# Chunk attention and feed-forward on one core: the first two tiles of attention in quadrant form, with their order written out step by step

## Chip, core and metric

One core of a Trainium2 chip runs the kernel alone. The metric is the device time of one execution in microseconds; the kernel before has a median of 288.91 us over 3 runs (288.83 to 289.1).

## What is computed

q, k and v have 8 batches, 8 heads, 576 rows and a head size of 64, in float32. Each head's rows are cut into 9 chunks of 64 and attention stays within a chunk. The heads are then joined to 4608 tokens of width 512, which go through a feed-forward network of width 2048 with an exact GELU.

```python
    scores = scale * np.matmul(q_c, k_c.transpose(0, 1, 2, 4, 3))
    ...
    attn = np.exp(scores)
    attn = attn / (np.sum(attn, axis=-1, keepdims=True) + 1e-09)
    out = np.matmul(attn, v_c)
    ...
    h = x @ w_in
    ...
    g = 0.5 * h * (1.0 + erf(h * inv_sqrt2))
    return (g @ w_out).astype(np.float32)
```

## The kernel before

**Tiles.** The work is 9 tiles of 512 tokens: tile t below 8 is the first 512 rows of batch t, tile 8 the last chunk of all batches. Heads go in 4 pairs g; the 512 columns of a pair are 8 chunks of 64. A tile has three parts: its attention, which gives x (128 x 4 x 512); mm1 (`mm1_slot`, L402), which makes the 16 slots f of h with 4 matmuls each over the slices ks of x, and the GELU on ScalarE (L405); and mm2 (`mm2_slot`, L418), which sums the 16 slots of h into 4 blocks of output rows. `phase(t)` runs mm1 and mm2 of tile t, and the attention of tile t+1 stands between its mm2 matmuls. For that, `extra2` says which pieces go ahead of which step. The program is a manual schedule: every engine works through its own queue in the order in which the program names its instructions.

**Attention of tiles 2 to 8** is in quadrant form (`quad_S`, `quad_av`): q and k are turned by a DMA transpose, V lies with keys on the partitions, and each matmul uses a 64x64 quarter of TensorE (L228, L280), so that four run at once. The change leaves it as it is.

**Attention of tile 0** comes first of all. SyncE issues the loads of q and k pair by pair (L114), then those of V (`load_v`, L163, eight DMAs into half of the partitions each), then w_in (L509). VectorE casts q to bfloat16 (L170) and GpSimd casts k and V (L170, L174). TensorE turns q and k by 128x128 transposes (L181); VectorE copies q out (L187). k goes into block-diagonal tiles k_bd, two copies of half the partitions on ScalarE (L194), and V into v_bd, so that a matmul over all 128 partitions does both heads of a pair (`att_S` L297, `att_av` L371). The zero blocks are memset by VectorE and GpSimd (L72 to L77). Row sums come from a matmul with ones (L305), a 32x32 transpose, a reciprocal and another transpose on VectorE (L309 to L314) for pairs 0 and 1, and from small matmuls (L349), a reciprocal (L352), float32 matmuls that spread it (L358) and a copy (L362) for pairs 2 and 3. VectorE multiplies A.V by the reciprocals into x (L373). `keep_warm` puts matmuls on zeros between them. Then come the casts of w_in (L512) and w_out (L520), shared by GpSimd and VectorE, and the first two f slots of mm1, slice by slice.

**Attention of tile 1** lies in tile 0's mm2, which there runs by h slot (`mm2_rows`, L472): for every f one matmul for each of the four row blocks, up to f 11, then by row block (L418). It has the same block-diagonal form, with the sums of pairs 1 to 3 in one bank (`att_sums`, L323). ScalarE carries the reciprocals over the partitions in small copies (L334). The last A.V stands between the first matmuls of tile 1's mm1, which does three f slots at once, in this order:

```python
        for ks in range(KS):
            for u in between.get(ks, ()):
                u()
            for a in range(n):
                nc.tensor.matmul(h_ps[a][:], w_in_sb[:, ks, (f + a) * P:(f + a + 1) * P], st["x"][:, ks, :],
                                 start=(ks == 0), stop=(ks == KS - 1))
```

**Buffers.** Every load lands in one of 6 stage tiles and waits for the casts that last read it. SyncE keeps at most eight of its DMAs in flight, since each waits for the eighth before it. TensorE's results use 8 banks, in three pools: `ps_mm` 3, `ps_tp` 2, `ps_at` 3.

## Time and profile before

| | |
|---|---|
| median of 3 runs | 288.91 us |
| profiled execution, own time | 289.0 us |
| its span | 287.2 us |
| TensorE, ScalarE, VectorE, GpSimd busy | 97%, 62%, 40%, 29% of the span |
| mm1 and mm2 matmuls (L402, L418, L472) | 576, 512 and 48, 379 ns each in the rows |
| DMA, read from HBM and written | 36.70 MB, 9.44 MB |

A matmul's row shows issue to end, and the next is issued before that end: in a steady stretch they follow each other every 0.216 us. In rows of a timeline the numbers are start, length, engine, line, operation, tiles and shape; in brackets stands the idle time before it and what ended that. Windows give per engine the busy time and the count of instructions, then the granted clock of TensorE, the mean busy share of the 16 DMA engines, and GB/s.

### The profile page before, as it was taken

What the parts mean: (1) busy time and instruction counts of PE and PEld (TensorE: products, weight loads), DVE (VectorE), ACT (ScalarE), POOL (GpSimd) and SP (SyncE); (2) the same over time, 40 slices, a digit from 0 to 9 for tenths busy, and PEclk for the clock granted to TensorE, in tenths of its full rate; (3) what the DMA queues carried; (4) which work ended last, traced back from release to release, by engine and by line L of the source; (5) the groups of instructions that cost most, each with busy time, mean ns of one, the idle gap of its engine ahead of it and who ended that gap; (6) DMA issues with size and microseconds to landing.
All of it is one profiled execution on the core that took longest, in us unless ns stands there. A gap on an engine that the chain in (4) does not pass through costs nothing.

```text
span 287.2 us, 5795 instructions
## 1 busy us (share of the span) xinstructions
PE 277.8 (97%) x2317; PEld 133.2 (46%) x2317; DVE 114.0 (40%) x209; ACT 176.8 (62%) x359; POOL 82.6 (29%) x134
## 2 busy tenths in 40 slices
PE   6699999999999999999999999999999999999995
PEld 2464455444444444444444444444444444444444
DVE  5855259504910491039202930293019401940011
ACT  3766757967647763677367737863686378646400
POOL 6759677511620620161005200620015020000000
PEclk9999999999999999999999999999999999999999
DMA  7999997999999926991698259924996490030033
GB/s 211 234 337 402 391 368 179 248 282 248 221 284 289 233 83 184 283 211 48 179 284 193 79 160 270 223 81 130 199 157 125 120 264 2 2 146 0 2 73 73
DMA packets 119435, 53.86 MB, mean 188 GB/s; under 512 B 97776, under 2 KB 112368, under 8 KB 119408
## 3 DMA queue, kind: packets, MB, share of 16 engines
q1 hardware_dynamic: 119248, 53.36, 71.0%
q8 instruction: 18, 0.29, 0.4%
q10 hardware_dynamic: 160, 0.13, 0.2%
q14 instruction: 9, 0.07, 0.1%
HBM read 36.70 MB, written 9.44 MB: 161 GB/s over the span
## 4 chain that ended last, share of the span: by engine, by line
PE 82%; DMA 10%; DVE 3%; SPq 1%; ACT 1%; issue 1%; POOL 0%; DVEq 0%
PE h_ps L402 38%; PE y_ps L418 38%; DMA arrival<-in_moe_w_out_dram 8%; DMA arrival<-in_k_dram 2%; PE s_ps L228 2%; PE av_ps L280 2%; PE y_ps L450 1%; SPq L114 1%; DVE x L373 1%; PE rc_ps L358 1%; DVE rc L341 1%; PE y_ps L472 1%; ACT k_bd L194 0%; ACT pT L299 0%; PE av_ps L371 0%
## 5 line engine op out<-in xcount | busy, mean ns | idle before, releaser
L402 PE MATMUL h_ps<-x,w_in_sb 128*128 128x512 bf16 x576 | 126.1, 379 | 0.7 <-POOL w_in_sb L512 0.6
L405 ACT ACTIVATE h<-h_ps 128x512 bf16<-128x512 f32 x144 | 85.5, 597 | 60.8 <-PE h_ps L402 60.7
L418 PE MATMUL y_ps<-w_out_sb,h 128*128 128x512 bf16 x512 | 113.8, 379 | 0.0
L402 PEld LDWEIGHTS <-w_in_sb 128*128 128x128 bf16 x576 | 56.2, 98 | 68.4 <-POOL w_in_sb L512 0.7
L418 PEld LDWEIGHTS <-h 128*128 128x128 bf16 x512 | 48.7, 98 | 57.0 <-issue 0.2
L246 DVE STREAM_TRANSPOSE pt<-pT 128x256 f32<-128x256 f32 x28 | 12.2, 437 | 106.8 <-ACT pT L235 106.8
L170 POOL CAST q_nat<-arrival 128x512 bf16<-128x512 f32 x31 | 18.0, 620 | 95.7 <-DMA arrival<-in_q_dram 71.8
L206 POOL CAST v_nat<-arrival 128x1024 bf16<-128x1024 f32 x14 | 14.5, 1040 | 39.5 <-DMA arrival<-in_v_dram 27.0
L536 ACT ACT_TABLE_LOAD x18 | 23.1, 1283 | 1.0 <-PEq L681 0.7
L433 DVE COPY y_sb<-y_ps 128x512 f32<-128x512 f32 x11 | 7.6, 690 | 36.7 <-PE y_ps L418 33.0
L259 ACT COPY part<-part 32x32 f32<-32x32 f32 x56 | 12.3, 219 | 15.0 <-DVE part L249 14.5
L287 DVE TENSOR_TENSOR x<-av_ps,rc 128x512 bf16<-128x512 f32 x28 | 18.9, 676 | 2.2
L249 DVE TENSOR_REDUCE part<-pt 128x16 f32<-128x512 bf16 x28 | 19.2, 685 | 1.0
L168 POOL CAST k_nat<-arrival 128x512 bf16<-128x512 f32 x28 | 16.2, 612 | 0.9 <-DMA arrival<-in_k_dram 0.8
L433 ACT COPY y_sb<-y_ps 128x512 f32<-128x512 f32 x24 | 13.8, 580 | 0.9
L235 ACT ACTIVATE pT<-s_ps 128x512 bf16<-128x512 f32 x28 | 14.3, 593 | 0.0
L472 PE MATMUL y_ps<-w_out_sb,h 128*128 128x512 bf16 x48 | 11.8, 379 | 0.4 <-POOL w_out_sb L520 0.4
L194 ACT COPY k_bd<-tp 64x512 bf16<-64x512 bf16 x12 | 6.9, 578 | 6.7 <-PE tp L181 6.5
L273 DVE STREAM_TRANSPOSE rc<-rb 128x512 f32<-128x512 f32 x14 | 9.9, 707 | 0.2
L273 DVE STREAM_TRANSPOSE rc<-across 128x512 f32<-128x512 f32 x14 | 9.8, 701 | 0.0
L174 POOL CAST v_bd<-arrival 64x512 bf16<-64x512 f32 x14 | 8.6, 615 | 0.7
L520 POOL CAST w_out_sb<-arrival 128x512 bf16<-128x512 f32 x10 | 6.7, 701 | 4.4 <-DMA arrival<-in_moe_w_out_dram 4.4
(76 smaller groups left out, 151.0 us busy)
## 6 DMA issues: line engine op xcount, KB each, us to landing
out_dram<-y_sb SPq DMA_DIRECT2D x32, 256.0 KB, 2.2
arrival<-in_v_dram SPq DMA_DIRECT2D x58, 128.0 KB, 3.4
arrival<-in_k_dram SPq DMA_DIRECT2D x28, 256.0 KB, 6.3
arrival<-in_q_dram SPq DMA_DIRECT2D x7, 1024.0 KB, 6.5
arrival<-in_moe_w_out_dram SPq DMA_DIRECT2D x4, 1024.0 KB, 12.9
arrival<-in_moe_w_in_dram SPq DMA_DIRECT2D x6, 512.0 KB, 7.1
arrival<-in_v_dram SPq DMA_DIRECT2D x28, 64.0 KB, 2.5
arrival<-in_q_dram SPq DMA_DIRECT2D x4, 256.0 KB, 5.0
```

Of the source, the lines that this page charges most:

```text
L168: copy(st[nm][:, :, g], st[nm + "f"][:, :, g].rearrange("p (q r) d -> p q r d", r=2))
L170: copy(st[nm][:, g].rearrange("p j r d -> p r j d"), st[nm + "f"][:, 2 * g:2 * g + 2])
L206: copy(st["v"][:, r::2], st["vf"][:, r::2])
L249: nc.vector.tensor_reduce(st["part", g2][:, c, :, :, 0], pt[:].rearrange("p n e u -> p n u e"), axis=mybir.AxisListType.X, op=mybir.AluOpT ...
L273: nc.vector.transpose(rc[:], tiles[t]["rb", g2][c].to_broadcast([P, NB, 32]))
L287: nc.vector.tensor_tensor(x.rearrange("p n (e u) -> p n e u", u=2), st["av"][g2][c][:].rearrange("p n (e u) -> p n e u", u=2), st["rc", 2 ...
L402: nc.tensor.matmul(h_ps[a][:], w_in_sb[:, ks, (f + a) * P:(f + a + 1) * P], st["x"][:, ks, :], start=(ks == 0), stop=(ks == KS - 1))
L405: nc.scalar.activation(st["h"][:, f + a, :], h_ps[a][:], Act.Gelu)
L418: nc.tensor.matmul(y_ps[:], st["h"][:, f, ms * P:(ms + 1) * P], w_out_sb[:, f, :], start=(f == 0), stop=(f == FF - 1))
L433: (AC if ms < 3 and t + 1 < NT else DV)(y_sb[:], y_ps[:])
L472: nc.tensor.matmul(tiles[t]["y_ps", ms][:], tiles[t]["h"][:, fi, ms * P:(ms + 1) * P], w_out_sb[:, fi, :], start=(fi == 0), stop=False)
L536: nc.scalar.activation(act_scratch[:], rest[:, 0:1], func)
```

## The change

- **Tiles 0 and 1 in quadrant form.** k stays dense: one copy out of the transposes (`att_T`) instead of two halves, and no k_bd, v_bd or memsets for them. `att_S` and `att_av` use 64x64 quarters. `att_S` takes one pair in tile 0 (16 matmuls, two Exp of 128x256), two in tile 1 (32 matmuls, two Exp of 128x512). V is loaded by head into all partitions (`load_v`) and cast by pair.
- **Reciprocals of two pairs.** `pair_sums` gives the sums of pairs 0 and 1 (tile 1: also 2 and 3) with two matmuls of 32 columns, one transpose and one reciprocal on half the partitions. `pair_over` spreads them with one float32 matmul, 128x32, where ScalarE copied; `pair_rc` makes the factors from that bank. In tile 0 pairs 2 and 3 keep small matmuls (`att_sums`, `att_spread`). The last step, `att_x`, is two instructions of half the width for each pair.
- **mm1 by slice.** `mm1_first` does the first f slots of tile 0 (two) and tile 1 (four, was three) ks by ks, with the last A.V between the slices: one pair in tile 0, two in tile 1.
- **Order.** Tile 0: GpSimd casts all of q and k and sets up four constants behind q 0 (`both` takes eight small copies); each piece is named where it is to run. SyncE issues V of heads 4 to 7 after the first half of w_in's first part; w_in's parts 2 and 3 are one DMA each; w_out's part 1 and tile 1's k come in halves. The stage has 7 tiles. Tile 1's pieces stand at other steps; ScalarE does all four y copies of tile 0; the fourth store of tile 0 follows V of tile 2.

The removed lines can be seen in the functions above; here stand the lines that are added and those kept between them.

```diff
+    both = consts.tile([P, P], f32, name="both")
+    nc.gpsimd.memset(both[:], 0.0)
+    for s in range(G):
+        for a in range(2):
+            at0 = CH * (s % 2) + QD * a
+            nc.gpsimd.tensor_copy(both[QD * s:QD * (s + 1), at0:at0 + QD], ident[QD * s:QD * (s + 1), QD * s:QD * (s + 1)])
...
-    stage = ctx.enter_context(tc.tile_pool(name="stage", bufs=6))
+    stage = ctx.enter_context(tc.tile_pool(name="stage", bufs=7))
...
+    def load_v(t, heads):
+        for h in heads:
+            nc.sync.dma_start(v_arrival(t)[:, h], v[t, h, 0:MT, :].rearrange("(n key) d -> key n d", key=P))
...
+    def att_T(t, nm, g, copy):
+        tp = ps_tp.tile([P, J, P], bf16, tag="tp", name="tp")
         for j in range(J):
+            nc.tensor.transpose(tp[:, j], tiles[t][nm][:, g, j].rearrange("p r d -> p (r d)"), ident[:])
+        to = work.tile([P, CT, CH], bf16, tag=nm + "T", name=nm + "T", bufs=4)
+        copy(to[:].rearrange("p i (c j) -> p i c j", j=J), tp[:].rearrange("p j (i c) -> p i c j", i=CT))
+        tiles[t][nm + "T", g] = to
...
+    def pair_sums(t, g2, pool, tag):
+        hold = slice(CH * g2, CH * (g2 + 1))
+        sum_ps = pool.tile([P, MT], f32, tag=tag, name="sums_ps")
+        for r in range(2):
+            at0 = CH * g2 + QD * r
+            nc.tensor.matmul(sum_ps[at0:at0 + QD], ones_c[:], tiles[t]["pT", 2 * g2 + r][:].rearrange("p u e -> p (u e)"),
+                             start=True, stop=True, tile_position=(0, at0))
+        t1 = work.tile([P, NB, 32], f32, tag="t1", name="t1", bufs=1)
+        nc.vector.transpose(t1[hold], sum_ps[hold].rearrange("p (n e) -> p n e", e=32))
+        r1 = work.tile([P, 2, NB], f32, tag="r1", name="r1", bufs=2)
+        nc.vector.reciprocal(r1[hold], t1[hold].rearrange("p n (c e) -> p c n e", c=2)[:, :, :, 0])
+        tiles[t]["r1", g2] = r1
+    def pair_over(t, g2, pool, tag):
+        hold = slice(CH * g2, CH * (g2 + 1))
+        rb = pool.tile([P, 2, NB], f32, tag=tag, name="rb_ps")
+        nc.tensor.matmul(rb[:], both[hold], tiles[t]["r1", g2][hold], start=True, stop=True, tile_position=(CH * g2, 0))
+        tiles[t]["rb", g2] = rb
+    def pair_rc(t, g2, c):
+        rc = work.tile([P, NB, 32], f32, tag="rc", name="rc", bufs=4)
+        nc.vector.transpose(rc[:], tiles[t]["rb", g2][:, c].to_broadcast([P, NB, 32]))
+        rows = rc[:].rearrange("p n e -> p (n e)").rearrange("p (u e) -> p u e", e=CH)
+        for g in (2 * g2, 2 * g2 + 1):
+            half = CT // 2
+            tiles[t]["rc", g, c] = rows[:, half * (g % 2):half * (g % 2 + 1)]
...
+    def att_S(t, gs, pool, tag):
+        st = tiles[t]
+        g2, half = gs[0] // 2, CT // 2
+        s_ps = [pool.tile([P, CT, CH], f32, tag=tag, name="s_ps") for _ in range(2)]
+        if gs[0] % 2 == 0:
+            for r in range(2):
+                st["pT", 2 * g2 + r] = work.tile([P, CT, CH], bf16, tag="pT", name="pT", bufs=5)
+        for g in gs:
+            for n in range(half):
+                for a in range(2):
+                    for r in range(2):
+                        c = a ^ r
+                        rs, cs = slice(CH * r, CH * (r + 1)), slice(CH * c, CH * (c + 1))
+                        nc.tensor.matmul(s_ps[r][cs, half * (g % 2) + n, :], st["kT", g][rs, 2 * n + c],
+                                         st["qT", g][rs, 2 * n + c], start=True, stop=True,
+                                         tile_position=(CH * r, CH * c))
+        for r in range(2):
+            u = slice(half * (gs[0] % 2), half * (gs[-1] % 2 + 1))
+            nc.scalar.activation(st["pT", 2 * g2 + r][:, u], s_ps[r][:, u], Act.Exp, scale=scale)
...
+    def att_sums(t, g, pool, tag):
+        st = tiles[t]
+        half = CT // 2
+        sT = pool.tile([P, half // 2, 2, 2], f32, tag=tag, name="sT")
+        for a in range(half // 2):
+            for r in range(2):
+                u = half * (g % 2) + 2 * a
+                nc.tensor.matmul(sT[:, a, r], st["pT", 2 * (g // 2) + r][:, u:u + 2].rearrange("p u e -> p (u e)"),
+                                 ones_r[:, 0:2], start=True, stop=True)
+        st["rr", g] = work.tile([P, half // 2, 2, 2], f32, tag="rr", name="rr", bufs=4)
+        nc.vector.reciprocal(st["rr", g][:], sT[:])
...
+    def att_spread(t, g, pool, tag):
+        st = tiles[t]
+        half = CT // 2
+        rc_ps = pool.tile([P, half, 2, CH], f32, tag=tag, name="rc_ps")
+        for a in range(half // 2):
+            for c in range(2):
                 for r in range(2):
+                    nc.tensor.matmul(rc_ps[CH * r:CH * (r + 1), 2 * a:2 * a + 2, c],
+                                     st["rr", g][:, a, r, c:c + 1].to_broadcast([P, D]), ident_f[:],
                                      start=True, stop=True, tile_position=(0, CH * r))
...
+    def att_av(t, g, pool, tag):
+        st = tiles[t]
+        half = CT // 2
+        if g % 2 == 0:
+            st["av", g // 2] = [pool.tile([P, CT, CH], f32, tag=tag, name="av_ps") for _ in range(2)]
+        av = [bank[:, half * (g % 2):half * (g % 2 + 1)] for bank in st["av", g // 2]]
+        st["av_of", g] = av
+        for n in range(half):
+            for r in range(2):
+                for c in range(2):
+                    cs, rs = slice(CH * c, CH * (c + 1)), slice(CH * r, CH * (r + 1))
+                    nc.tensor.matmul(av[c][rs, n], st["v"][cs, 2 * g + r, n],
+                                     st["pT", 2 * (g // 2) + r][cs, half * (g % 2) + n, :], start=True, stop=True,
+                                     tile_position=(CH * c, CH * r))
+    def att_x(t, g):
+        x = tiles[t]["x"][:, g, :].rearrange("p (n c e) -> p n c e", c=2, e=CH)
+        for c in range(2):
+            nc.vector.tensor_tensor(x[:, :, c], tiles[t]["av_of", g][c], tiles[t]["rc", g, c], op=mybir.AluOpType.mult)
...
+    def mm1_first(t, banks, steps):
+        st = tiles[t]
+        st["h"] = hpool.tile([P, FF, MT], bf16, tag="h", name="h")
+        h_ps = {}
+        for step in steps:
+            if callable(step):
+                step()
+                continue
+            fs, kss = step
+            for ks in kss:
+                for f in fs:
+                    if ks == 0:
+                        pool, tag = banks[f]
+                        h_ps[f] = pool.tile([P, MT], f32, tag=tag, name="h_ps")
+                    nc.tensor.matmul(h_ps[f][:], w_in_sb[:, ks, f * P:(f + 1) * P], st["x"][:, ks, :],
+                                     start=(ks == 0), stop=(ks == KS - 1))
+        for f in range(len(banks)):
+            nc.scalar.activation(st["h"][:, f, :], h_ps[f][:], Act.Gelu)
...
+        load_v(0, range(0, 4))
+        win_load, win = zip(*(load_w_in(c, 2 if c < 2 else 1) for c in range(NWC)))
+        win_load[0](0)
+        load_v(0, range(4, H))
+        win_load[0](1)
+        for a in range(2):
+            win_load[1](a)
+        for c in range(2, NWC):
+            win_load[c](0)
...
+        qk_in(0, "q", 0, PO, DV)
+        qk_in(0, "k", 0, PO, AC)
+        keep_warm(3)
+        qk_in(0, "q", 1, PO, DV)
         cast_qk(0, "k", 1, PO)
+        att_S(0, (0,), *at)
+        att_T(0, "k", 1, AC)
+        keep_warm(2)
+        qk_in(0, "q", 2, PO, DV)
+        att_S(0, (1,), *at)
+        qk_in(0, "k", 2, PO, AC)
+        keep_warm(2)
+        qk_in(0, "q", 3, PO, DV)
+        pair_sums(0, 0, *mm)
         cast_qk(0, "k", 3, PO)
+        att_S(0, (2,), *at)
+        att_T(0, "k", 3, AC)
         keep_warm(3)
+        pair_over(0, 0, *mm)
+        pair_rc(0, 0, 0)
+        cast_v(0, 0, PO)
+        cast_v(0, 1, PO)
+        att_S(0, (3,), *at)
+        att_av(0, 0, *tp)
+        att_sums(0, 2, *mm)
+        pair_rc(0, 0, 1)
+        att_av(0, 1, *tp)
+        win[0](0, PO)
+        att_sums(0, 3, *at)
+        att_spread(0, 2, *mm)
+        att_x(0, 0)
+        cast_v(0, 2, PO)
+        win[0](1, PO)
+        att_av(0, 2, *at)
+        att_spread(0, 3, *mm)
         act_table(Act.Gelu)
+        att_x(0, 1)
+        cast_v(0, 3, PO)
+        att_x(0, 2)
+        def last_x():
+            att_av(0, 3, *at)
+            att_x(0, 3)
+            win[0](2, PO)
+            win[0](3, DV)
+        mm1_first(0, (mm, mm), (((0, 1), (0,)), last_x, ((0, 1), (1, 2, 3))))
...
+        def later_casts():
+            cast_qk(1, "k", 2, DV)
+            cast_qk(1, "k", 3, PO)
+        def w_out_casts():
+            for i in range(FC):
+                wout[2](i, DV if i % 2 == 0 else PO)
+            for i in (0, 2):
+                wout[3](i, PO)
+            for g in range(G):
+                cast_v(1, g, PO)
...
+        phase(0, {0: [lambda: act_table(Act.Exp)], 2: Tq[0:2], 3: Tq[2:3], 4: Tq[3:4] + Tk[0:1],
+                  5: Tk[1:2] + [later_casts], 6: [lambda: att_S(1, (0, 1), *at)],
+                  7: Tk[2:4] + [w_out_casts, next_qk],
+                  8: [lambda: pair_sums(1, 0, *at), lambda: att_S(1, (2, 3), *tp), lambda: act_table(Act.Gelu)],
+                  9: [lambda: pair_over(1, 0, *at), lambda: pair_rc(1, 0, 0), lambda: pair_rc(1, 0, 1)]
+                     + [lambda i=i: wout[3](i, AC) for i in (1, 3)],
+                  10: [lambda: pair_sums(1, 1, *tp)],
+                  11: [lambda: pair_over(1, 1, *tp), lambda: pair_rc(1, 1, 0)],
+                  12: [lambda: att_av(1, 0, *at), lambda: att_x(1, 0), lambda: pair_rc(1, 1, 1)],
+                  14: [lambda: att_av(1, 1, *at), lambda: att_x(1, 1)]},
+              by_rows=True, first=2)
         pool_cast_qk(2)
+        mm1_first(1, (mm, mm, mm, at),
+                  (((0, 1, 2, 3), (0,)), lambda: (att_av(1, 2, *tp), att_x(1, 2)), ((0, 1, 2, 3), (1,)),
+                   lambda: (att_av(1, 3, *tp), att_x(1, 3)), ((0, 1, 2, 3), (2, 3))))
```

## The prediction

> **What bounds the kernel now.** I read the busy table of the page first, then TensorE's waits, then the timelines of TensorE, SyncE and VectorE up to 55 us and the half-microsecond windows of the start.
>
> ```profile
> span 287.2 us, 5795 instructions
> ...
> PE 277.8 (97%) x2317; PEld 133.2 (46%) x2317; DVE 114.0 (40%) x209; ACT 176.8 (62%) x359; POOL 82.6 (29%) x134
> ```
>
> The reader is to see that TensorE is busy 277.8 of 287.2 us, so at most some 9 us can be won by filling its idle time. The rest is won only by giving it less to do. From tile 2 on the change leaves the order as it is, and the chain of waits shows nothing but matmuls there (a slot of 64 in 13.81 us, 0.2157 each). So the sum needs two clocks only: when TensorE begins f slot 2 of tile 0, and when it has done four f slots of tile 1.
>
> ```profile
> 17.17 0.64 PE L371 MATMUL av_ps<-pT,v_bd 128*128 128x64 bf16 x16
> 18.37 2.98 PE L402 MATMUL h_ps<-x,w_in_sb 128*128 128x512 bf16 x13 [0.56 <-POOL w_in_sb L512]
> ```
>
> This is TensorE's timeline. All of tile 0's attention ends at 17.6, then the first feed-forward matmul waits until 18.37, for a cast of w_in which itself waited for its load (the GpSimd casts of it start at 17.71 and 18.99). Its eight matmuls of f 0 and 1 end at 18.37 + 8 x 0.2157 = **20.10**.
>
> ```profile
> 4.84 7.64 SPq L163 DMA_DIRECT2D arrival<-in_v_dram  x8
> 12.53 6.56 SPq L509 DMA_DIRECT2D arrival<-in_moe_w_in_dram  x7
> ```
>
> ```profile
> 9.00:10.50 1.50, 1.19 (x19) 0.74 (x18) 1.07 (x3) 0.99 (x3) 0.88 (x2) 1.00 1.25 281
> 10.50:12.00 1.50, 0.79 (x12) 0.53 (x10) 1.43 (x3) 1.38 (x3) 1.10 (x2) 1.00 0.67 152
> 12.00:13.50 1.50, 0.90 (x19) 0.60 (x18) 1.47 (x4) 1.46 (x3) 1.32 (x4) 1.00 0.79 182
> 13.50:15.00 1.50, 1.26 (x26) 0.82 (x24) 1.31 (x5) 0.79 (x2) 1.38 (x3) 1.00 0.97 260
> ```
>
> The first two lines are SyncE's issues, the others windows (last columns: granted clock, DMA share, GB/s). V's eight issues hold the queue until 12.5, and transfers fall to 152 to 182 GB/s between 281 and 260. The last V issues took 0.64 us for 128 KB each, 205 GB/s: the dip is the issue of 256-byte pieces, and w_in stands behind it.
>
> ```profile
> 41.92 1.02 PE L472 MATMUL y_ps<-w_out_sb,h 128*128 128x512 bf16 x4 [0.44 <-POOL w_out_sb L520]
> ...
> 46.60 0.40 PE L323 MATMUL sums_ps<-pT,ones_c 128*32 128x512 bf16 x4
> 46.93 1.04 PE L418 MATMUL y_ps<-w_out_sb,h 128*128 128x512 bf16 x4
> ```
>
> Tile 1's attention lies between tile 0's mm2 matmuls. That stretch runs from 32.19 to 55.07 (four f slots of tile 1 done): 22.9 us, of which 80 matmuls at 0.2157 are 17.26, transposes 1.78, scores and A.V eight groups of 0.233, sums 0.22 and 0.43, and 1.2 are stalls counted from issue to issue (0.60 for w_out, 0.30 for the last x, 0.32 for transposes).
>
> **The change, step by step: the start.** The same q and k loads land at the same times, the last k at 10.85. GpSimd now casts all of them (0.57 each, spacing of its runs of four). After q0 (3.62 to 4.19) come 13 small constants, worked out from the 0.14 spacing of the small memsets at L57 to L65: 1.9 us (ends: 1.3 at their 0.10 each, 3.8 at the 0.29 of the 128x128 cast), so k0 is cast at 6.1 to 6.7, not 5.5; by q2 the casts wait for loads again, and k3 is done at 11.5 as before. The v_bd and k_bd memsets that go were in the shade of the loads: nothing.
> I then walked the queues in program order with before's rows: transposes 0.22 for four, VectorE copy 0.62, ScalarE copy 0.55, an Exp pair of half width 0.66 (a full one costs 0.54 to 0.60, the smallest activation 0.20), 0.2 from a matmul's issue to its reader. The second Exp ends at 10.9, the pair's sums at 11.4, transpose and reciprocal at 12.8, rb at 13.1. From there **VectorE is the bound**: from 13.29 it holds two rc transposes of 0.66, two reciprocals of 0.25, 0.4 of waiting, and four x of 0.67 (two halves; two full x took 1.29, so a half is 0.33), and ends at 18.17. TensorE does ks 3 at 18.27 and begins f 2 at **18.71** instead of 20.10: 1.4 earlier. f 0 and 1 now run between the last A.V and VectorE's x, and their w_in is cast at 15.6.
> Loads: 512 KB of w_in among V's pieces can fill the dip, (290 - 170) GB/s for 3.5 us = 0.42 MB, at 320 GB/s 1.3 us. So I take w_in's second to fourth half 1.3 us earlier than the casts that waited for them (18.96, 20.92, 22.18), at 17.6, 19.6, 20.9, and the third and fourth megabyte, each one DMA now, at 23.5 and 26.1. f 8 needs its slice at 23.9 and gets it at 24.03: a stall of 0.15. mm1 ends at 30.93 instead of 32.19: **1.26 us gained**. If the dip is not filled, the third megabyte lands at 24.8 (before's halves: 23.46, then between that and 27.45) and the gain is 0: that is its lower end; the upper is 1.4 and the dearest row gone, 1.7.
>
> **Tile 1.** The unknown is what a group of quadrant matmuls (64x64) costs between full-array ones. Nearest row:
>
> ```profile
> 65.53 0.74 PE L228 MATMUL s_ps<-q_t,k_t 64*64 64x64 bf16 x64
> 66.20 6.22 PE L418 MATMUL y_ps<-w_out_sb,h 128*128 128x512 bf16 x28
> ```
>
> The matmul before it is issued at 65.22, so it is over at 65.44: 0.09 pass before the group, and 66.20 - 65.44 = 0.76 in all. Inside, four quadrants go every 0.0316, 16 x 0.0316 = 0.51. So 0.26 is paid for going in and out. The four sums at 46.60 (32-column strips, all at once) give 0.09 + 0.11 = 0.20. I take 0.23 a group and keep 0 (below nothing there is no reason) and 0.26 as ends. The cheaper arithmetic is thus eaten: a score pair costs 0.25 + 0.23 = 0.48 against 2 x 0.233, an A.V of one pair 0.13 + 0.23 = 0.36 against 0.233.
> [...]
> Sum after: 17.26 + 1.78 + scores 0.94 + two sums 0.84 + two rb 0.52 (float32, 128x32; between 0.2 and the 0.3 of L358's first pair) + four A.V 1.43 = 22.8, against 21.6 before. Stalls: w_out's third megabyte lands 1.3 to 1.8 us earlier and is cast at 40.6, before f 8 at 41.0, so the 0.60 goes; but rb must wait for VectorE's 0.68 transpose and 0.34 reciprocal: 0.2 for the first, and 0.5 for the second, which stands behind two rc of 0.66 in VectorE's queue, with f 11 behind it on TensorE; with smaller ones 0.85. The stretch becomes 23.6: **0.73 lost**.
> V of tile 1 and the last w_out are cast by GpSimd and ScalarE just before use: A.V of pair 0 comes at 46.1 and needs the first two heads landed by 45.4; I hold them at 43.7 (before: the first V casts start at 46.26).
> With one answer, nothing: the seventh stage buffer, w_out in halves, the Gelu table before the last sums, the last store of tile 0 behind V of tile 2 on SyncE's queue (tile 2's operands are wanted at 65), and all four y copies on ScalarE. The cover of these copies is thin: the third ends at 50.2, and f 2 of tile 1 wants its bank at 50.7; what it is late is lost.
>
> **Sum.** 1.26 - 0.73 = 0.53 earlier, and nothing downstream to give it back: 289.0 - 0.5 = 288.5 for an execution like the profiled one (span 287.2, 1.8 around it). The median shown is 0.09 below that execution: **288.4**.
>
> **A place to check.** TensorE now idles 2.0 us from 4.7 to 6.7, against 0.7 at most before. The first seven warm matmuls took 0.43 apart, later ones 0.216; the windows grant 1.00 throughout. If idling brought the 0.43 back for a while, each four transposes would cost 0.2 more, and the first 3 us of mm1 up to 1.5 more.
> [...]
>
> **Rivals.** (1) A larger gain. For: the ends of the unknowns, 0.23 free in all groups gives 0.53 + 1.15 = 1.7; a dip that is filled and casts that meet it. Against: the 0.76 row. 288.91 - 1.5 = 287.4.
> (2) **Slower: V of tile 1 comes late.** V's and w_out's last loads queue behind one another, eight DMAs in flight, and before the last w_out landed only at 45.1 although its neighbours came 2.5 apart. With TensorE's order fixed, A.V of pair 0 blocks everything behind it. Landing 2.0 us later than I hold costs 0.3, 2.6 costs 0.9, 3.5 about 1.8 in all: 288.4 + 1.5 = 289.9. It decides from a landing of the first two heads at about 46.6, one microsecond later than before. Against it: w_in and w_out keep their order and have one more stage buffer.
> (3) The start isn't shorter: the dip stays, or GpSimd's constants take 3 us and shift the chain by 1.1 us; then tile 1's 0.7 eats what is left: 289.1. This is also the case that the change does not do what it says.
>
> **Chances.** As walked (288.4, from 287.9 to 288.9) 0.43; larger gain 0.25; no shorter start 0.14; late V 0.18. A difference of 0.2%, 0.58 us, is about what a measurement can tell from none, so faster means under 288.33: all of the second case and somewhat less than half of the first, 0.25 + 0.20 = 0.45. Slower, over 289.49: the late V and a little of the third, 0.19. The rest, 0.36, lies between. The range reaches from the rival's 287.4 less 0.4 for the bounds to 290.0, beyond the late V.
>
> **What would show it.** The start is right if f 2 begins near 18.7 and VectorE is busy from 13 to 18 without a break; wrong if the first feed-forward matmuls wait for w_in or the dip in GB/s is still there. Tile 1 is right if each A.V of 16 matmuls takes 0.33 to 0.39 and rb twice holds TensorE for VectorE; wrong if quadrant groups cost no more than their 0.13, or a wait for v_nat stands at A.V. The forecast fails if TensorE idles over 0.5 us anywhere between 20 and 54 for a load.

## The result and the profile after

The changed kernel takes **291.91 us** (median of 4 runs, 291.28 to 292.68) against 288.87 us of the kernel before on the same chip: ratio 1.0107, 95% interval 1.0080 to 1.0134. It is 3.0 us slower where 0.5 less was forecast, and 1.9 above the 290.0 at which the forecast's range ended. The profiled execution took 292.15 us with a span of 290.3.

The busy table of the page after:

```profile
span 290.3 us, 6047 instructions
...
PE 280.5 (97%) x2453; PEld 133.4 (46%) x2453; DVE 105.4 (36%) x204; ACT 170.2 (59%) x344; POOL 75.0 (26%) x130
```

TensorE is busy 2.7 us longer than before, and idle 0.4 longer. Both have to be looked for by stage. Four marks cut the profiled executions: the begin of f slot 2 of tile 0 (f 2), the end of tile 0's mm1, the first mm2 matmul of tile 1, and the end of the last matmul. All rows of this study in one table, "rest" being from tile 1's first mm2 matmul to the last matmul (us; the ratio is of all timed runs to those of before on their chip):

| kernel | f 2 | mm1 end | mm1 end to tile 1's mm2 | rest | span | ratio [95%] |
|---|---|---|---|---|---|---|
| before | 20.10 | 32.19 | 34.01 | 217.47 | 287.2 | 1 |
| after | 21.82 | 33.91 | 34.85 | 217.94 | 290.3 | 1.0107 [1.0080, 1.0134] |
| r1_after_again | 21.83 | 33.92 | 34.85 | 218.81 | 291.2 | 1.0156 [1.0118, 1.0194] |
| e1_consts_vector | 21.31 | 33.39 | 34.85 | 218.43 | 290.3 | 1.0154 [1.0129, 1.0179] |
| e2_warm_early | 19.75 | 31.89 | 35.66 | 218.20 | 289.4 | 1.0096 [1.0073, 1.0120] |
| e3_count_up | 20.55 | 32.64 | 35.27 | 217.47 | 289.0 | 1.0098 [1.0075, 1.0121] |
| e4_vector_no_warm | 20.51 | 32.59 | 35.42 | 217.50 | 289.1 | 1.0111 [1.0089, 1.0133] |
| e5_vector_v_first | 20.34 | 32.43 | 35.43 | 217.62 | 289.1 | 1.0119 [1.0084, 1.0154] |
| e6_tile1_late | 22.35 | 34.44 | 34.33 | 218.14 | 290.5 | 1.0084 [1.0053, 1.0115] |
| e7_both | 21.35 | 33.45 | 34.47 | 218.25 | 289.8 | 1.0106 [1.0074, 1.0139] |
| e8_mended | 20.10 | 32.18 | 34.34 | 217.47 | 287.6 | 1.0085 [1.0054, 1.0116] |
| e9_before_four_more | 20.61 | 32.69 | 34.90 | 217.46 | 288.6 | 1.0029 [1.0007, 1.0051] |
| e10_mended_halves | 19.44 | 31.52 | 34.80 | 217.45 | 287.5 | 1.0107 [1.0062, 1.0152] |

(For before and e9, whose rows don't split there, f 2 is the mm1 end less 56 x 0.2157.) From before to after the span grows by 3.14: 1.72 in the start, 0.84 in tile 1, 0.47 in the rest, 0.11 behind the last matmul. The forecast had 1.26 gained, 0.73 lost, 0 and 0. So tile 1 is as forecast, and the start is off by 3 us in this profile.

TensorE's timeline of the start, after:

```profile
4.43 0.40 PE L166 MATMUL tp<-ident,q_nat 128*128 128x128 bf16 x4
7.42 0.43 PE L166 MATMUL tp<-ident,k_nat 128*128 128x128 bf16 x4 [2.60 <-POOL k_nat L155]
7.66 1.47 PE L529 MATMUL warm<-rest 128*128 128x512 bf16 x3
...
18.96 0.32 PE L358 MATMUL av_ps<-pT,v_nat 64*64 64x64 bf16 x16
20.52 1.47 PE L384 MATMUL h_ps<-x,w_in_sb 128*128 128x512 bf16 x6 [1.24 <-issue]
21.82 12.25 PE L395 MATMUL h_ps<-x,w_in_sb 128*128 128x512 bf16 x56
```

Three things are to be seen. TensorE idles 2.60 us for k0. The three warm matmuls behind that take 1.47, 0.43 apart, where warm ones later in the kernel go every 0.216. And ahead of ks 1 it stands for 1.24 us with "issue" as the reason: it waits for nothing that the profile names.

GpSimd's timeline of the kernel after tells of the first:

```profile
3.76 0.61 POOL L155 CAST q_nat<-arrival 128x512 bf16<-128x512 f32 x1 [2.20 <-DMA arrival<-in_q_dram]
4.31 0.30 POOL L52 CAST ident_f<-ident 128x128 f32<-128x128 bf16 x1
4.55 1.57 POOL L58 CAST both<-ident 32x32 f32<-32x32 bf16 x8
6.18 0.23 POOL L62 MEMSET ones_r<- 64x1 bf16 x2
6.44 0.25 POOL L66 MEMSET ones_c<- 64x16 bf16 x2
6.75 0.61 POOL L155 CAST k_nat<-arrival 128x512 bf16<-128x512 f32 x1
```

The windows of the same kernel tell of the second (columns: length, TensorE busy, granted clock, DMA share, GB/s):

```profile
4.24:7.65 3.41, 0.75 (x9) 1.00 0.97 297
7.65:11.07 3.42, 3.42 (x33) 0.50 1.22 281
```

The 13 constants take 2.4 us (4.31 to 6.75) with k0's cast behind them, although k0 landed at 4.38; and GpSimd had idled 2.20 for q0 with the constants queued behind q0's cast. In the 3.41 us in which TensorE was busy only 0.75, it still had its full clock; in the next 3.41 us it had half of it.

This fall is not in every execution. The record lists the mean clock of each: one fall of 3.41 us in a span of 290 makes 0.994 of it, an estimate. Of the eight executions of this kernel (four here, four in r1) five show it, with a mean span of 290.8, and three had their full clock, with 290.4; of the 32 of the kernel before that are listed with the experiments, one. So the half clock is seen at f 2 in a profile, but it does not tell this kernel's longer executions from its shorter ones, and those with the full clock (289.9 to 290.9) still lie above all of before's (285.7 to 287.6).

In tile 1 of the kernel after, TensorE's timeline has the forecast's lines:

```profile
44.84 0.40 PE L233 MATMUL rb_ps<-r,both 64*128 64x32 f32 x2
...
47.88 0.38 PE L233 MATMUL rb_ps<-r,both 64*128 64x32 f32 x2 [0.37 <-DVE r L226]
48.19 1.04 PE L470 MATMUL y_ps<-w_out_sb,h 128*128 128x512 bf16 x4
49.16 0.32 PE L358 MATMUL av_ps<-pT,v_nat 64*64 64x64 bf16 x16
49.41 1.90 PE L453 MATMUL y_ps<-w_out_sb,h 128*128 128x512 bf16 x8
```

An A.V of a pair takes 0.36 from the end of the matmul before it (49.05) to the begin of the next (49.41); the second rb waits for VectorE's reciprocal.

### The profile page after: what moved, and what is told of

The parts are those of the page before. It is cut to its first block, busy times and chain, and to the rows that moved or that the text cites. A ratio compares the mean times of both kernels' runs of the same rounds, so it can differ in the third digit from the quotient of the medians.

```text
span 290.3 us, 6047 instructions
## 1 busy us (share of the span) xinstructions
PE 280.5 (97%) x2453; PEld 133.4 (46%) x2453; DVE 105.4 (36%) x204; ACT 170.2 (59%) x344; POOL 75.0 (26%) x130
## 4 chain that ended last, share of the span: by engine, by line
PE 94%; DVE 1%; POOL 1%; issue 1%; DMA 1%; ACT 0%; POOLq 0%
PE h_ps L395 41%; PE y_ps L410 37%; PE y_ps L470 3%; PE h_ps L384 2%; PE av_ps L284 2%; PE s_ps L203 2%; PE tp L166 1%; PE y_ps L453 1%; PE y_ps L439 1%; DMA arrival<-in_q_dram 1%; PE warm L529 1%; PE rc_ps L338 1%; PE s_ps L310 1%; PE av_ps L358 1%; POOL both L58 0%
## 5 line engine op out<-in xcount | busy, mean ns | idle before, releaser
L395 PE MATMUL h_ps<-x,w_in_sb 128*128 128x512 bf16 x552 | 120.6, 379 | 0.0
L397 ACT ACTIVATE h<-h_ps 128x512 bf16<-128x512 f32 x138 | 82.4, 597 | 60.2 <-PE h_ps L395 60.2
L410 PE MATMUL y_ps<-w_out_sb,h 128*128 128x512 bf16 x496 | 109.7, 379 | 0.0
L395 PEld LDWEIGHTS <-w_in_sb 128*128 128x128 bf16 x552 | 54.0, 98 | 65.3 <-issue 0.3
L410 PEld LDWEIGHTS <-h 128*128 128x128 bf16 x496 | 47.3, 98 | 55.8
L155 POOL CAST q_nat<-arrival 128x512 bf16<-128x512 f32 x35 | 20.5, 624 | 94.7 <-DMA arrival<-in_q_dram 89.8
L263 ACT COPY part<-part 32x32 f32<-32x32 f32 x56 | 12.2, 219 | 15.0 <-DVE part L253 14.6
L424 DVE COPY y_sb<-y_ps 128x512 f32<-128x512 f32 x10 | 6.9, 691 | 35.3 <-PE y_ps L410 35.3
L470 PE MATMUL y_ps<-w_out_sb,h 128*128 128x512 bf16 x48 | 12.2, 380 | 0.0
L507 POOL CAST w_in_sb<-arrival 128x512 bf16<-128x512 f32 x9 | 6.6, 742 | 7.5 <-DMA arrival<-in_moe_w_in_dram 7.5
L315 ACT ACTIVATE pT<-s_ps 128x256 bf16<-128x256 f32 (+1 forms) x12 | 4.8, 452 | 6.1 <-PE s_ps L310 6.1
L529 PE MATMUL warm<-rest 128*128 128x512 bf16 x17 | 7.1, 553 | 1.2 <-DVE rest L47 1.2
```

The costliest lines, as they stand in the source:

```text
L155: copy(st[nm][:, g].rearrange("p j r d -> p r j d"), st[nm + "f"][:, 2 * g:2 * g + 2])
L395: nc.tensor.matmul(h_ps[:], w_in_sb[:, ks, f * P:(f + 1) * P], st["x"][:, ks, :], start=(ks == 0), stop=(ks == KS - 1))
L397: nc.scalar.activation(st["h"][:, f, :], h_ps[:], Act.Gelu)
L410: nc.tensor.matmul(y_ps[:], st["h"][:, f, ms * P:(ms + 1) * P], w_out_sb[:, f, :], start=(f == 0), stop=(f == FF - 1))
L424: (AC if t == 0 or ms < 3 and t + 1 < NT else DV)(y_sb[:], y_ps[:])
L470: nc.tensor.matmul(tiles[t]["y_ps", ms][:], tiles[t]["h"][:, fi, ms * P:(ms + 1) * P], w_out_sb[:, fi, :], start=(fi == 0), stop=False)
```

## The experiments

**Theory A**: GpSimd's constants hold k0's cast, TensorE idles, and the idling costs it its clock. **Rival B**: the new attention's own work makes the start late. **Theory C**: the 1.24 us are a wait for TensorE's own instructions; **rival D**: for some data that the profile doesn't name. To theory C belong the trace's records of an instruction queue (q8): 19 transfers of 16,384 bytes in the kernel after, 18 in before. That they carry TensorE's instructions, some 256 each, is an estimate from the 4,900-odd matmuls and weight loads in after; one of them lands at 19.24, and TensorE resumes at 20.52.

**e1_consts_vector.** The constants' code, each `nc.gpsimd` made `nc.vector`:

```diff
-    nc.gpsimd.tensor_copy(ident_f[:], ident[:])
+    nc.vector.tensor_copy(ident_f[:], ident[:])
...
```

> The changed kernel, with its 13 small constants (ident_f, both, ones_r, ones_c) built by VectorE instead of GpSimd, so that k0's cast stands right behind q0's. Theory A (the start is late because these constants hold k0's cast 2.4 us, TensorE then idles from 4.83 to 7.42 and is granted half its clock from 7.65 to 11.07): k0 is cast about 2 us earlier, TensorE never idles 2 us, the granted clock stays 1.00 in all half-microsecond windows, the first Exp pair comes 1.3 to 1.7 us earlier, f 2 begins at 20.1 to 20.5 instead of 21.82, and the time is 290.2 to 290.8. Rival B (the start is late by the work of the new attention itself, 32 float32 spreads at 1.09 for 16 and x by halves on VectorE; the slow clock lay beside waits for loads): the clock is mended, f 2 stays at 21.5 to 21.9, and the time is 291.6 to 292. Both keep the 1.24 us of idle ahead of ks 1.

k0 was cast at 4.39, and the second group of scores came 2.7 us earlier than in the kernel after (8.73 instead of 11.41). Yet f 2 began only 0.5 earlier, and the time did not fall: 292.57, ratio 1.0154. Neither theory had it. TensorE's timeline in e1 shows one new thing:

```profile
16.40 0.43 PE L358 MATMUL av_ps<-pT,v_nat 64*64 64x64 bf16 x16 [1.55 <-POOL v_nat L161]
```

The windows of e1 show another (columns: length, busy time of all five engines, granted clock, DMA share, GB/s):

```profile
12.76:16.17 3.41, 2.00 (x68) 1.55 (x52) 2.63 (x8) 1.24 (x3) 1.22 (x3) 1.00 1.01 219
16.17:19.58 3.41, 3.18 (x34) 1.99 (x34) 0.76 (x2) 0.78 (x2) 1.91 (x4) 0.50 1.03 314
```

The chain now meets V's second half, which stands behind half a w_in slice and landed at 15.2 to 16.7; and after that wait the clock falls again, at 16.17 now, over the last A.V and the first matmuls of mm1. In e1's three other executions it did not fall (0.3 to 0.7 us longer than this one), so the fall isn't why the time stayed. The 1.24 us of idle ahead of ks 1 is gone, though both expectations had it stay.

**e2_warm_early.** All ten later warm matmuls ahead of k0's transposes:

```diff
+        keep_warm(10)
         qk_in(0, "k", 0, PO, AC)
-        keep_warm(3)
...
```

> The changed kernel, with its ten later warm matmuls all put ahead of k0's transposes, so that they fill the idle stretch; GpSimd's constants stay ahead of k0's cast and TensorE has the same number of instructions. It parts the two halves of theory A. If the half clock is what costs: granted clock 1.00 throughout, transposes 0.22 for four instead of 0.43, f 2 at 20.6 to 21.1, time 290.7 to 291.2. If the late cast of k0 alone costs: clock mended, f 2 within 0.3 of 21.82, time 291.6 to 292. Rival B as well: 291.6 to 292.

The clock is 1.00 throughout, f 2 is at 19.75 with k0 as late as ever. So the late cast of k0 alone doesn't make f 2 late. How much of the gain is the clock's can't be read here: the edit also takes ten warm matmuls out of the chain behind k0, and the stall ahead of ks 1 is gone with it. The time gains less, 291.09. Tile 1 gives 0.81 of it back (35.66 instead of 34.85). Lines of the chain of waits there:

```profile
30.18 11.20 DMA arrival<-in_moe_w_out_dram
41.38 0.02 issue
41.40 1.18 DVE w_out_sb L518 x2
42.58 0.63 DVE t L224
...
43.63 0.42 PE rb_ps L233 x2
```

The third megabyte of w_out lands at 41.38, in before at 41.20, in the kernel after at 41.49: it takes no notice of when the start ends. Two casts of it stand in VectorE's queue ahead of the pair's transpose, and rb waits 0.64 for them.

**e3_count_up.** Sixteen tiny matmuls more ahead of k0's transposes, in the idle time:

```diff
+        count_up(16)
         qk_in(0, "k", 0, PO, AC)
```

> The changed kernel with 16 tiny matmuls (128x2, 32 more TensorE instructions) ahead of k0's transposes. Theory C (the 1.24 us in which TensorE issues nothing ahead of ks 1 are a wait for the next 256 of its own instructions, whose 16 KB transfer lands at 19.24): the stall keeps its place in the count of instructions, so it now stands 16 matmuls earlier in the work, ahead of the last A.V or within it, and ks 1 follows ks 0 without it; the time changes by less than 0.5 us either way. Rival D (the idle belongs to what stands there: ks 1 waits for x, or for a cast of w_in, that the trace doesn't name): it stays ahead of ks 1 with 1.0 to 1.3 us.

The half clock stays (7.79 to 11.20), and the stall is gone from the start altogether. TensorE's timeline:

```profile
18.88 0.32 PE L358 MATMUL av_ps<-pT,v_nat 64*64 64x64 bf16 x16
19.35 1.36 PE L384 MATMUL h_ps<-x,w_in_sb 128*128 128x512 bf16 x5 [0.16 <-issue]
```

(Where one matmul is short in the count, as here, the 0.16 is its missing record.) So D falls: the same data, the same order, no wait. C as written falls too, since the stall did not move 16 matmuls up; here the transfer started at 14.61 instead of 17.91. Against the kernel after, mm1 ends 1.27 earlier. That the place alone doesn't make the stall is seen in e1 and e2 too, which have the kernel after's count of instructions and no stall there.

**e4_vector_no_warm.** The constants as in e1, and the ten later warm matmuls left out.

> The constants on VectorE, as in e1_consts_vector, and the ten later warm matmuls left out (20 TensorE instructions fewer ahead of f 2). Theory C: the place of the instruction wait moves 10 matmuls later, into mm1's 128x512 matmuls, which are long enough to hide most of it as in the kernel before, so f 2 begins 0.8 to 1.2 us earlier than in e1_consts_vector, at 19.0 to 19.6, and the time is 289.0 to 289.8. Rival D: f 2 as in e1_consts_vector within 0.3, same time. If the granted clock falls below 1.00 without the warm matmuls, f 2 comes later than in e1_consts_vector by theory A, 0.5 to 1.5 us.

The clock fell at 7.78 for 10.2 us, and f 2 came at 20.51: neither the 19.0 to 19.6 of theory C nor later than in e1, as the last sentence had it for this case, but 0.80 earlier. Behind q's second pair, for which it waits 1.65, TensorE waits for no load, and it has no stall of instructions. That the chain keeps pace with the loads at half the clock is a reading of it and not shown, since the ten warm matmuls and e1's wait for V are gone as well. The time is 291.51.

**r1_after_again.**

> The changed kernel as it is, profiled a second time, since the 1.24 us of idle ahead of ks 1 stood in none of the four kernels tried so far. Theory C in its first form (a fixed place in the count of instructions): the idle stands there again with 1.0 to 1.3 us, f 2 at 21.8. Theory C', an instruction transfer that comes late in some executions and not in others: f 2 at 20.4 to 20.8 without it, or the stall somewhere else. By both k0 is cast at 6.75, TensorE idles 2 us or more, the clock falls to half for about 3.4 us, and the median is 1.008 to 1.013 times that of before.

The first form of C: the stall is back, in the same place, as a line of TensorE's timeline.

```profile
20.75 1.24 PE L384 MATMUL h_ps<-x,w_in_sb 128*128 128x512 bf16 x5 [1.61 <-issue]
```

It belongs to this kernel, then, not to one execution. The row counts five of six matmuls: the first has no record, and TensorE resumed some 0.22 before the row, at about 20.5, after about 1.4 us. And the rest of the span holds a second one, in tile 7's A.V. TensorE's timeline there, of the kernel after:

```profile
220.77 0.66 PE L284 MATMUL av_ps<-pT,v_nat 64*64 64x64 bf16 x58
221.74 0.25 PE L284 MATMUL av_ps<-pT,v_nat 64*64 64x64 bf16 x6 [0.31 <-issue]
```

The same view of this execution:

```profile
221.03 0.66 PE L284 MATMUL av_ps<-pT,v_nat 64*64 64x64 bf16 x58
222.61 0.25 PE L284 MATMUL av_ps<-pT,v_nat 64*64 64x64 bf16 x6 [0.92 <-issue]
```

It stands behind matmul 58 or 59 of the 64 in six of the seven kernels and executions with this count of instructions (after, r1, e1, e2, e6, e7), and in none with another count. And TensorE resumes 1.28 to 1.63 us after the landing of an instruction transfer:

| place | transfer lands | TensorE resumes | between |
|---|---|---|---|
| start, after | 19.24 | 20.52 | 1.28 |
| start, r1 | 19.14 | about 20.5 | about 1.4 |
| tile 7, after | 220.37 | 221.74 | 1.37 |
| tile 7, r1 | 221.19 | 222.61 | 1.42 |
| tile 7, e1 | 220.19 | 221.71 | 1.52 |
| tile 7, e2 | 219.16 | 220.79 | 1.63 |
| tile 7, e6 | 220.48 | 221.97 | 1.49 |
| tile 7, e7 | 219.75 | 221.21 | 1.46 |

In profiles without the stall (e3, e5, e8) it had landed 1.5 us or more ahead of the place, which is 16 matmuls further up in e3 and e8. So theory C is the reading that is left, in its second form: a place fixed by the count, and a transfer that comes late or not. The stall's cost is shown, by e3, which is without it; that it is a wait for instructions is argued, from these eight landings. Why it starts at 17.9 and 18.0 in these two starts and at 12.0 to 14.6 in the others was not found.

**e5_vector_v_first.** e1 with V's eight loads in one piece ahead of w_in:

```diff
-        load_v(0, range(0, 4))
+        load_v(0, range(0, H))
...
-        load_v(0, range(4, H))
...
+        cast_v(0, 2, PO)
+        cast_v(0, 3, PO)
         win[0](0, PO)
```

> Constants on VectorE as in e1_consts_vector, and all eight loads of V again ahead of w_in's first half (GpSimd casts V's heads ahead of w_in). Theory L (the loads come at a fixed rate, so which half stands first only chooses who waits): V's last heads land by 14.5, the A.V of pair 2 waits no longer (1.55 us in e1_consts_vector), TensorE keeps its full clock, but f 2 needs the second half of w_in's first megabyte, which lands at 18.4 to 18.9 as in every kernel so far, so f 2 begins at 19.3 to 19.9 and mm1 ends at 31.4 to 32.0; time 290.4 to 291.2, about 1.5 under e1_consts_vector. Rival M (the start is bound by the attention's own chain, which ends 1.5 to 2 earlier once no V is awaited): f 2 at 18.3 to 18.8, mm1 end by 31, time under 290.2.

V is awaited no longer, and the clock stays at 1.00. Instead TensorE's timeline shows w_in:

```profile
17.79 0.39 PE L384 MATMUL h_ps<-x,w_in_sb 128*128 128x512 bf16 x1 [1.29 <-POOL w_in_sb L507]
...
20.34 12.25 PE L395 MATMUL h_ps<-x,w_in_sb 128*128 128x512 bf16 x55
```

M falls, by 1.5 us and more. L had a wait for w_in, but for the second half of its first megabyte; the one awaited is the first half, which now stands behind V and landed at 17.06 (14.01 in the kernel after). L was 0.4 too early for f 2 and mm1's end and 0.5 too low for the time: 291.70, by ratio 1.0119 against e1's 1.0154 on another chip.

**e6_tile1_late.** e2 with the second pair's rb moved behind the first A.V, and w_out's casts away from VectorE's front:

```diff
-            for i in range(FC):
-                wout[2](i, DV if i % 2 == 0 else PO)
+            for i, eng in ((0, AC), (1, PO), (3, PO)):
+                wout[2](i, eng)
...
-                  9: [lambda: pair_over(1, 0, *at), lambda: pair_rc(1, 0, 0), lambda: pair_rc(1, 0, 1)]
+                  9: [lambda: pair_over(1, 0, *at), lambda: wout[2](2, DV), lambda: pair_rc(1, 0, 0), lambda: pair_rc(1, 0, 1)]
...
-                  11: [lambda: pair_over(1, 1, *tp), lambda: pair_rc(1, 1, 0)],
-                  12: [lambda: att_av(1, 0, *at), lambda: att_x(1, 0), lambda: pair_rc(1, 1, 1)],
+                  12: [lambda: att_av(1, 0, *at), lambda: att_x(1, 0), lambda: pair_over(1, 1, *tp), lambda: pair_rc(1, 1, 0), lambda: pair_rc(1, 1, 1)],
```

> e2_warm_early with two edits in tile 1: the second pair's rb matmuls one step later (behind the first A.V), and two casts of w_out's third megabyte taken from ahead of the first pair's transpose on VectorE (one to ScalarE, one behind it). Theory T (tile 1's attention costs 0.6 to 0.8 more than it need, because TensorE waits twice at rb for VectorE, 0.64 and 0.37 in e2_warm_early): both waits are under 0.1, the stretch from the end of tile 0's mm1 to tile 1's first mm2 matmul falls from 35.66 to 34.5 to 34.8, and the time is 0.8 to 1.1 under e2_warm_early: 290.0 to 290.3. Rival L' (TensorE waits for the third megabyte of w_out, which lands at 41.4 in all kernels, whatever stands at rb): the waits move to f 8 or f 10 of mm2 and the stretch stays within 0.3.

Both waits are gone, as TensorE's timeline shows, and the stretch is 34.33, just under what T gave, where L' had it stay at 35.66. That is 0.52 under the kernel after's. Part of the fall from e2 is not the edits': this start ends at 34.44, 2.55 later than e2's, and w_out's third megabyte was there sooner by as much. Starts that end alike settle it: e8 with the edits has 34.34 at mm1 end 32.18, e4 and e5 without them 35.42 and 35.43 at 32.59 and 32.43.

```profile
45.37 0.41 PE L233 MATMUL rb_ps<-r,both 64*128 64x32 f32 x2
...
49.08 0.41 PE L233 MATMUL rb_ps<-r,both 64*128 64x32 f32 x2
```

The time is 290.53, ratio 1.0084. Its start is that of e2 in code, but in this execution the clock fell (windows: all engines, clock, DMA share, GB/s):

```profile
11.32:14.73 3.41, 2.51 (x86) 2.05 (x86) 2.88 (x8) 1.79 (x5) 1.81 (x4) 1.00 1.13 286
14.73:18.14 3.41, 2.43 (x38) 1.97 (x36) 1.86 (x6) 0.58 (x1) 1.86 (x4) 0.50 1.02 291
```

f 2 is at 22.35, against 19.75 in e2's profile. Of the ten executions that have this start (four of e2, six of e6), the clock fell in this one alone, the longest of e6's six (span 290.5, the others 288.0 to 288.9); so its row in the table is not e6's usual one.

**e7_both.** e5 with e6's two edits in tile 1, and without e2's order of the warm matmuls.

> e5_vector_v_first with the tile 1 edits of e6_tile1_late. If theories L and T both hold, mm1 ends at 31.4 to 32.0, tile 1's stretch is 34.5 to 34.9, tile 1's first mm2 matmul begins at 66.0 to 66.8 where before has 66.20, and the time is within 0.8 of before's. If M and T hold it is 0.5 to 1.5 faster than before. If neither edit is worth what it is held at, it stays over 1.006 times before.

Tile 1 takes 34.47, as T has it; the start ends at 33.45, since w_in's second half came later in this execution (TensorE waits 1.17 for it ahead of f 2), and so did the loads behind it: w_out's third megabyte is cast from 42.90 on, against 41.74 in e5. The ratio, 1.0106, is that of the last sentence, though the tile 1 edit was worth what T held it at.

**e8_mended.** The kernel after with all later warm matmuls kept, the idle time filled with more, and e6's tile 1:

```diff
+        keep_warm(8)
+        count_up(8)
         qk_in(0, "k", 0, PO, AC)
```

> The changed kernel with both places mended at once: eight warm and eight tiny matmuls more fill TensorE's idle ahead of k0's transposes (all later warm matmuls stay, 32 TensorE instructions more in all, the count of e3_count_up, which showed no stall of instruction supply), and the tile 1 edits of e6_tile1_late. If the half clock, the supply stall and the rb waits are the losses: clock 1.00 throughout, f 2 at 19.6 to 20.0 (V's second half and w_in's second half, landing at 18.5 to 18.9, set that), mm1 end 31.7 to 32.2, tile 1's first mm2 matmul at 66.1 to 66.7 (66.20 in before), the rest 217.5, span 287.1 to 287.9, time 0.998 to 1.003 times before. If a loss is missing from the list, the span stays over 288.5.

The profiled execution is within the expectation but for f 2, which is 0.1 late: span 287.6, clock 1.00, no stall of instructions, no wait at rb in tile 1. Its start is exactly before's: f 2 at 20.10, mm1 end at 32.18. What is left in it is V:

```profile
16.61 0.32 PE L358 MATMUL av_ps<-pT,v_nat 64*64 64x64 bf16 x16 [0.63 <-POOL v_nat L161]
...
20.10 12.25 PE L395 MATMUL h_ps<-x,w_in_sb 128*128 128x512 bf16 x56
```

The timed runs do not follow: median 290.36, ratio 1.0085, with spans from 287.6 to 290.1, where the expectation ended at 1.003. The profiled execution is the shortest of the five, and all five, the 290.1 too, had their full clock (0.998 or more).

**e9_before_four_more.** The kernel before with `count_up(4)` ahead of its `keep_warm(3)`.

> The kernel before, with four tiny matmuls (128x2, eight TensorE instructions) in an idle place of the start, so that tile 7's group of 128 A.V instructions ends 2 instructions ahead of a 256-instruction boundary (counted from the stall in the changed kernel's start), as in the changed kernel, instead of 10 ahead. Theory C' (a late instruction transfer is hidden only by the slow 128x512 matmuls that stand between the small ones and the boundary): the stretch from tile 1's first mm2 matmul to the last matmul grows from 217.47 by 0.3 to 1.2, all of it around 214 to 222, and the time by as much. Rival (the 0.5 to 1.3 us lost there come from the changed loads, stores or casts): 217.4 to 217.6, time as before within 0.3.

No stall: the rest is 217.46. The boundary's place had been counted from the program's list alone, which leaves out some of TensorE's instructions between the start and tile 7: between its two stalls the trace of the kernel after has 1788 matmuls, 3576 with a weight load each (1796 loads are recorded), and 14 of the transfers begin (17.91 to 193.28), hence 255 to 256 each, an estimate; 14 x 256 is 3584. With some 8 to 14 more, an estimate, the place lies inside the A.V group in this run, and at its end or just behind it in before already. There the transfer starts 3.0 to 3.9 us ahead of the group, in the kernels that stall 1.3 to 1.8. So this run says that the count alone doesn't make a stall. It does not make one where it was meant to, so it does not confirm theory C either. The 0.3% is not the rest's: this profile, the longest of the run's ten executions, lost 0.5 in the start and 0.9 in tile 1, there waiting for w_out, whose third megabyte is cast from 42.64 on (41.25 in before).

**e10_mended_halves.** e8 with w_in's third megabyte in two halves:

```diff
-        win_load, win = zip(*(load_w_in(c, 2 if c < 2 else 1) for c in range(NWC)))
+        win_load, win = zip(*(load_w_in(c, 2 if c < 3 else 1) for c in range(NWC)))
...
```

> e8_mended with w_in's third megabyte loaded in two halves again, as before does. Theory L (the loads' total rate caps the start and tile 1, whatever their pieces): the third megabyte of w_out lands at 41.1 to 41.6 as in all kernels, time as e8_mended within 0.4. Rival (one DMA of 1 MB is slower than two of half, which is why the lead of half a microsecond at 20 us is gone by 27 us): w_in's last megabyte lands at 26.5 to 26.9 instead of 27.3, w_out's third 0.4 to 0.8 earlier, and the time falls by up to 0.3.

w_in's last megabyte lands at 27.14 and w_out's third at 41.28: the rival falls. The profiled execution has the earliest start of all (f 2 at 19.44, mm1 end 31.52), with no wait for V or w_in in it, and tile 1 takes 0.46 more than in e8, so that its mm2 comes only 0.20 earlier. The chain of waits tells why; it now begins with tile 1's q:

```profile
19.97 12.90 DMA arrival<-in_q_dram
32.87 0.05 issue
32.92 0.88 POOL q_nat L155
33.81 0.05 issue
33.85 0.40 PE tp L166 x4
```

The time is inconclusive: 291.61 with an interval of 0.9%.

**c1_before_look, c2_before_look, c3_mended_look, c4_mended_look**: before twice, and e8 twice, unchanged.

> The kernel before, profiled again: its executions have spans from 285.7 to 287.6 us, and the profile worked with so far (287.2) stands near their upper end. Theory V (what varies is how early the weight loads and the V loads land, which both kernels wait for in the first 50 us): from tile 1's first mm2 matmul to the last matmul it is 217.4 to 217.6 again, and all of the difference to 287.2 stands ahead of it, in the waits for w_in (0.56) and w_out (0.44). Rival W (instruction transfers or the clock vary): the difference stands behind it, or as waits for nothing the profile names.

> As c1_before_look, a second look at the kernel before: theory V has both looks agree within 0.2 from tile 1's first mm2 matmul on and differ, if at all, in waits for loads ahead of it; rival W has them differ behind it.

> e8_mended, profiled again: its spans ranged from 287.6 (the one profiled) to 290.1. Theory V: an execution that takes longer shows it ahead of tile 1's first mm2 matmul, as waits for v_nat, w_in or w_out, 0.5 to 2 us, with the clock at 1.00. Rival W: it shows the clock at one half for 3.4 us or more in the start, or 0.5 to 1.5 us in which TensorE waits for no semaphore (in the start or at 214 to 222), with its instruction transfer landing late.

> As c3_mended_look, one more execution of e8_mended: by theory V 0.5 to 2 us more in waits for loads than in the first profile, by rival W in the clock or in waits for instructions; if it has a span of 287.4 to 287.9 again it tells nothing.

The spans are 287.4, 287.1, 287.9 and 288.0; the rest is 217.60, 217.57, 217.59 and 217.48. The mended kernel's 0.3 to 0.4 over its first profile goes with V (waits for v_nat of 1.0 in all, against 0.63), with 0.12 in the rest in c3 and 0.28 in tile 1 in c4. That agrees with V, and so do the profiles of e7 and e9, in which the loads came 1.2 and 1.4 later at w_out's third megabyte; but none of the mended kernel's long executions was caught. The clock half of W is answered for the longest ones by the list of executions: e8's 290.1 and e10's 291.4 had their full clock (1.0 and 0.999). The other half, waits for instructions, stays open. **Open**: in profiles the mended kernel is 0.6 us over before (mean of three each), in timed runs 2.0 by the medians and 2.4 by the ratio. Where the timed runs lose the other 1.4 to 1.8 us is in no profile.

## Why the prediction was wrong

- **GpSimd's constants, 1.9 us, k0 cast at 6.1**: 2.4 us and 6.75. The place was right, the size 0.5 short: a 32x32 copy takes 0.20, not the 0.14 of a small memset. The upper end (3.8) held it.
- **"A place to check", costed at nothing**: this step failed in the profile. The idle time was 2.60 us instead of 2.0, and the clock fell to half for 3.41 us. e8 and e10 give TensorE the same work as e3 from k0's transposes on, at full clock: f 2 at 20.10 and 19.44 against 20.55, so the half clock cost 0.45 (e8 waits 0.63 for V) to 1.11 (e10 waits for no load). The half pace was named there with a price of up to 1.5, and then left out of sum and rivals. In the kernel's time it can't be seen, since three of the eight executions had no fall and are hardly shorter. The prediction's line that the windows grant 1.00 throughout misled here: the trace of before has no clock record ahead of 5.04, and its transposes go at half pace up to about there (0.107 apart at 4.45, 0.056 at 5.59). That an idle stretch of 2.0 us costs nothing, as the sum has it, is shown by no run. In the kernel after the gap of 2.60 (4.82 to 7.42) lay in 3.41 us of full clock with TensorE busy 0.75 (4.24 to 7.65), and half the clock followed until 11.07.
- **VectorE as the bound, f 2 at 18.71**: in no run. VectorE's chain from its first transpose of rc to the last x took 5.2 us against 4.9 forecast (14.99 to 20.15), so its length was right, but it began 1.7 late in the kernel after. Where the delay was mended, V or w_in was awaited in e1, e2, e5 and e8. e10 waited for neither and still came at 19.44, 0.73 late, with k0's cast 0.65 late.
- **Loads: a filled dip worth 1.3 us**: this step failed too. The windows after (all engines, clock, DMA share, GB/s):

```profile
9.00:10.50 1.50, 1.50 (x26) 1.14 (x25) 0.69 (x1) 0.54 (x2) 1.49 (x4) 0.50 1.30 253
10.50:12.00 1.50, 1.50 (x27) 0.91 (x26) 0.49 (x1) 0.82 (x3) 0.83 (x2) 0.81 1.18 258
12.00:13.50 1.50, 1.50 (x30) 0.90 (x28) 0.96 (x3) 1.08 (x4) 0.69 (x2) 1.00 1.17 302
13.50:15.00 1.50, 1.18 (x19) 0.56 (x20) 0.91 (x3) 0.97 (x3) 0.62 (x1) 1.00 1.23 210
```

  The dip is filled, 258 and 302 GB/s where before had 152 and 182, and a smaller one opens behind it (210 for 260). The lead is 0.5 us when w_in's first megabyte is in (18.47 against 18.94), 1.0 at the next half (19.92, 20.90), and 0.1 at w_in's end (27.36, 27.45). w_out's third megabyte is even 0.3 later. From 21 to 42 us the windows of 3 us carry 364 to 408 GB/s in both kernels, so what was gained at 12 us was not kept. And V's second half, which the half slice of w_in was put ahead of, is what e1, e2 and e8 then wait for (1.55, 0.43 and 0.25, 0.63).
- **1.26 us gained at mm1's end (30.93)**: 1.72 lost in the profile. The distance of 2.98 is, by single profiles: 1.27 the stall ahead of ks 1 (e3), 0.46 to 1.12 the half clock (mm1 end of e8 and e10 against e3), and the remaining 0.59 to 1.25 is put down to the wait for V, which e8 has and e10 hasn't, and to k0's cast, 0.65 later than the earlier of the two times forecast.
- **Nothing about TensorE's instructions**: the part that no step and no rival had. The stall with no named releaser is 1.24 and about 1.4 in the start of the two profiles, and the rest is 0.47 and 1.34 longer than before's, where the sum said "nothing downstream to give it back".
- **Tile 1, 23.6 with 0.73 lost**: right, 23.73 (33.91 to 57.64), and by its own parts. A.V 0.36 as worked out, no wait for w_out, rb waits 0 and 0.45 between the matmuls around it (0.2 and 0.5 forecast). V's first heads landed at 44.9 to 45.4, not at 43.7, and still in time. The late-V rival did not occur in tile 1. Part of this is luck: the sum had w_out's third megabyte 1.3 to 1.8 earlier than in before, it came 0.3 later, and it was not awaited only because the start was 3 us behind the forecast. Two sums are loose and did not matter: the parts named for before's 22.9 add to 22.75, and rival 1's 1.15 "in all groups" is 0.23 five times, where its sum lists two sums, two rb and four A.V beside the scores.
- **What was missed there**: the 23.6 holds for a late start only. With mm1 over at 31.9 to 32.6, tile 1 took 35.27 to 35.66 (e2 to e5, without the edits), so that up to 0.8 of the better start was given back. No version beat before.

**What was shown and what not.** That the stall ahead of ks 1, the half clock and rb's waits cost time in a profiled execution is shown, the first and the last by runs without them, the half clock within the bounds above. That V and w_in cap the start is shown for e1, e5 and e8, which wait for one or the other, and not for e10; that w_out and q set tile 1's end behind an early start is shown by e2 and e10. c1 says the same of before: its mm1 ends 0.58 later than in the first profile, and tile 1 is 0.51 shorter. In the timed runs all mends together (e8) bring the ratio from 1.0107 to 1.0085 only. So the step that failed is the start: f 2 at 18.71 and mm1's end at 30.93, worked out with a lead that the loads keep and with no stall and no slow clock on TensorE; the eleven rows of the table that have the change show 19.44 to 22.35 and 31.52 to 34.44. But which of its parts makes up most of the 3 us in the timed runs is open, and so is the mended kernel's remaining 0.85%; that this too comes from the loads is only argued.
